# Output tiles of a second layer moved to other places in on-chip memory: four places for even chunks, four for odd ones, and a fifth store tile

## The chip, the core and the metric

The kernel runs on one core of a Trainium2 chip. A core has a matrix engine (PE), three elementwise engines (DVE, ACT, POOL) and a queue that only issues transfers (SP); each engine works through its own instructions strictly in order and waits on semaphores. SBUF is the on-chip memory of 128 partitions, and a tile takes the same range of bytes in each of them. The metric is device time in microseconds (us), the median of several runs; lower is better.

## The reference, cut to what matters

The input is one sequence of 4096 rows of 640 numbers. A modulation vector is made from `c`; then come a spectral block and a gated feed-forward block, each added to the residual:

```python
sa, ca, ga, sb, cb, gb = (silu(c) @ w_mod) cut in six
h = layernorm(x) * (1 + ca) + sa
x = x + ga * A(h)
h = layernorm(x) * (1 + cb) + sb
x = x + gb * ((silu(h @ w_gate) * (h @ w_up)) @ w_down)

def A(x):                              # along the 4096 rows
    z = rfft(x), its 640 channels cut in 4 blocks of 160
    h = relu(z @ w1 + b1)              # complex, per block
    o = h @ w2 + b2                    # complex, per block: the "second layer"
    o = sign(o) * max(|o| - 0.01, 0)   # real and imaginary part apart: "shrink"
    return irfft(o)
```

## The kernel before

**The spectral block, first part.** The transform of 4096 is split in 128 x 32. The input lies in eight tiles `xa0` to `xa7` (pool `xp`), each 10240 bytes of a partition, one after the other. Each is normalized, multiplied on PE by the constant `fa`, copied back over itself, and stored to memory by `write_s1(t, f)` in three shares f = 0, 1, 2 of its rows; I call such a store (t, f). These stores stand in SP's queue among loads, in the order of the code: (5,1), (0,1), (6,1), (7,1), (5,2), load of `g2` and `tb2`, (6,2), (7,2), and last (0,2); then the small constants `idn`, `tx`, `bx`, and then the first rows of `w_mod` (`wm`, L543). A tile's place is free for others when its stores have landed.

**The chunks.** The frequencies are worked in eight chunks `ch`, each with four channel blocks `b`, all in an order written out by hand; a step `p` is 4·ch + b. `stage_b` (L631, tile `pb`) is the second half of the transform; `evac_b` and `evac_r` copy it out as `z` and `rz` (ACT L638 and L661, DVE L639 and L671); `stage_l1` (L727, `pl`) is the first layer, whose results ACT (L744, L745) and DVE (L746, L759) take to `h` and `u`; `stage_l2` (L795, `pc`; for the first block also L792 and L806) is the second layer. DVE adds its bias and writes the sum to the output tiles `tts[ch, q, b // 2]` (named tt or tu): L807 for the first block, L797 for all others. `shrink_parts` (ACT L815 into the scratch tile `cl`, L816 in place) and `shrink` (DVE L819) apply the threshold. `stage_i` (L837, `pi`) is the first half of the inverse transform with the constant `bx`; ACT copies it to the four store tiles `co` (L840), which go to memory (`s2`) by POOL's queue (L845, and L843 for the last chunk). `first_blocks` runs chunk 0 and starts chunk 1; the loop over p follows.

Tiles that `stage_l2`, `shrink` and `stage_i` use lie in pool `p2`, which is laid over the places of `xp`. Who uses a place first waits for whoever used it before; the framework derives these waits from addresses. In bytes of a partition:

| place of | bytes | pool `p2` before |
|---|---|---|
| xa0 | 116672–126912 | nothing |
| xa1 | 126912–137152 | acc, cl, wx, bx, start of w2a |
| xa2, xa3 | 137152–157632 | w2a, w2b, start of w2c |
| xa4 | 157632–167872 | end of w2c, first tt place (chunk 0: q 0, b 0 and 1) |
| xa5 | 167872–178112 | four tt places (two used in chunk 0) |
| xa6 | 178112–188352 | a tt place (chunk 0: q 1, b 0 and 1), wm, two co places |
| xa7 | 188352–198592 | two co places, xn0, xn1 |

**The feed-forward block.** Its pool `fp` is laid over the same bytes. Its first step, `first_g`, transposes four normalized rows (`pt`, L1875), and per k writes the high part `ht` (ACT L1877), a copy `hx` (ACT L1880 for k < 3, DVE L1882 for the others) and the low part (DVE L1883); PE multiplies in the order k by k (L1889, L1890 with the high part, L1891 with the low one, tile `pg`). `hx0_0` lies at 186368, where before the last chunk's store tiles `co7_2` and `co7_3` lie. After that PE runs almost without a pause to the end (row 350.00:1451.00 of the prediction).

Of the kernel before, what the change touches and what calls it, by code (L numbers as in the profile page):

```python
# [6 lines left out]
F32 = mybir.dt.float32  # L7
# [6 lines left out]
P = 128  # L14
D = 640
# [151 lines left out]
def body(tc, x, w1, b1, w2, b2, wg, wu, wd, c, wm, k_fa, k_tb, k_tx, k_bx, k_ga, k_ge, k_id, out, dbg=None):  # L167
# [29 lines left out]
    with ExitStack() as top:  # L197
# [34 lines left out]
        with ExitStack() as af:  # L232
# [288 lines left out]
            p2 = af.enter_context(tc.tile_pool(name="p2", bufs=1, side="right", reuse_waits="tile"))  # L521
# [96 lines left out]
            tts = {}  # L618
# [154 lines left out]
            def stage_l2(ch, b, then=()):  # L773
                h0, h1, r2, _ = hss[ch, b]
                late = []
                de = slice(160 * (b % 2), 160 * (b % 2) + 160)
                for q in range(3 if ch == CE else 2):
                    fs = slice(128 * q, 128 * q + 128) if q < 2 else slice(256, 258)
                    M = 128 if q < 2 else 2
                    W = 320 if q < 2 else 160  # L780
                    if b % 2 == 0 and q < 2:
                        tts[ch, q, b // 2] = p2.tile([P, 2, 320], F32, tag="tt", bufs=6, name=f"tt{ch}_{q}_{b // 2}")
                    pc = ps.tile([P, 512], F32, tag="p2" if q < 2 else "p1", name=f"pc{ch}_{b}_{q}")
                    seq = [(h0[:, 0, fs], w2a[:, b, 0:W]), (h0[:, 1, fs], w2a[:, b, 0:W]),
                           (h0[:, 0, fs], w2a[:, b, 320:320 + W]),
                           (h1[:, 0, fs], w2b[:, b, 0:W]), (h1[:, 1, fs], w2b[:, b, 0:W]),
                           (h1[:, 0, fs], w2b[:, b, 320:320 + W]),
                           (r2[:, fs], w2c[:, b, 0:W]), (r2[:, fs], w2c[:, b, 320:320 + W])]
                    if (ch, b) == (0, 0):
                        late.append((pc, [seq[k] for k in (2, 5, 7)]))  # L790
                        for i, k in enumerate((0, 1, 3, 4, 6)):
                            mm(pc[:M, :W], *seq[k], start=(i == 0), stop=False)  # L792
                        continue
                    for i, (l, m) in enumerate(seq):
                        mm(pc[:M, :W], l, m, start=(i == 0), stop=(i == len(seq) - 1))  # L795
                    if q < 2:
                        dve.tensor_tensor(tts[ch, q, b // 2][:, :, de], pc[:, :320].rearrange("p (r e) -> p r e", r=2),  # L797
                                          b2t[:, :, b, :], op=OP.add)
                        if then:
                            then[q]()  # L800
                    else:

                        dve.tensor_tensor(tts[ch, 0, b // 2][0:1, 1, de], pc[0:1, :160], b2t[0:1, 0, b, :], op=OP.add)
                for q, (pc, seq) in enumerate(late):
                    for i, (l, m) in enumerate(seq):
                        mm(pc[:, :320], l, m, start=False, stop=(i == 2))  # L806
                    dve.tensor_tensor(tts[ch, q, b // 2][:, :, de], pc[:, :320].rearrange("p (r e) -> p r e", r=2),  # L807
                                      b2t[:, :, b, :], op=OP.add)

            cos = {}  # L810
# [14 lines left out]
            def stage_i(ch, hf, tag=("p1", "p1", "p3", "p3")):  # L825
                e = slice(320 * hf, 320 * hf + 320)
                if hf == 0:
                    cos[ch] = [p2.tile([P, D], F32, tag="co", bufs=4, name=f"co{ch}_{j}") for j in range(4)]
                co = cos[ch]
                pi = [ps.tile([P, 512], F32, tag=tag[j], bufs=1 if tag[j][0] == "b" else 2, name=f"pi{ch}_{hf}_{j}")  # L830
                      for j in range(4)]
                for r in range(2):
                    for q in range(2):
                        for j in range(4):
                            k = slice(32 * j, 32 * j + 32)
                            kd = 0 if 4 * ORDER[ch] + j + q == 0 else 1
                            mm(pi[j][64 * q:64 * q + 64, :320], bx[k, kd, r, :], tts[ch, q, hf][k, r, :],  # L837
                               start=(r == 0), stop=(r == 1))
                for j in range(4):
                    act.activation(co[j][:, e], pi[j][:, :320], AF.Copy)  # L840
                    m = 4 * (4 * ORDER[ch] + j)
                    if ch == NCH - 1:
                        (pool if hf else nc.scalar).dma_start(s2[m:m + 4, :, e].rearrange("k n d -> (k n) d"), co[j][:, e])  # L843
                    elif hf:
                        pool.dma_start(s2[m:m + 4].rearrange("k n d -> (k n) d"), co[j])  # L845

            on = lambda f, p, *a: f(p // 4, p % 4, *a) if 0 <= p < NP else None
            inverse = lambda p: stage_i(p // 4, p % 4 // 2) if p >= 0 and p % 2 == 0 else None

            e32 = hp.tile([P, 5, 2], F32, name="e32")  # L850
# [29 lines left out]
            def first_blocks():  # L880
# [19 lines left out]
                stage_l1(0, 2, later)  # L900
                stage_b(0, 3)
                stage_l2(0, 0)
                evac_b(0, 3)
                evac_rh(0, 3)
                stage_l2(0, 1, (lambda: evac_rl(0, 3), lambda: None))
                for f in later:
                    f()
# [5 lines left out]
                tail_l1(0, 3)  # L913
                evac_r(1, 0)
                stage_l2(0, 2)
                stage_b(1, 1)
                evac_b(1, 1)
# [5 lines left out]
            for p in range(LAST + 1):  # L923
                ch, b = p // 4, p % 4
# [75 lines left out]
            for p in range(LAST + 1, NP):  # L1000
                if p == LAST + 1:
                    on(shrink, p - 4)
                elif p == LAST + 3:
                    on(shrink_v, p - 3)
                    on(shrink_v, p - 2)
                on(stage_l1, p)
                on(tail_l1, p)
                if p < LAST + 3:
                    on(shrink_v, p - 3)
                if p == LAST + 1:  # L1010
                    load_first_rows(rb - 16, rb, nc.sync)
                elif p == LAST + 2:
                    load_first()
                    first_gate()
                for f, *a in sums.get(p, ()):
                    f(*a)
                if p == LAST + 1:
                    stage_i(NCH - 2, 0)
                on(stage_l2, p - 1)
                if p == LAST + 2:  # L1020
                    stage_i(NCH - 2, 1)
                    load_first_rows(rb, rb + 16, nc.sync)
# [74 lines left out]
        with ExitStack() as ff:  # L1097
# [15 lines left out]
            for n, (k, p) in enumerate(WG):  # L1113
                STG.append(("w", n))
                if k == "g" and p:
# [26 lines left out]
            bufs = {"R": 2, "h1": 1, "wb": 2, "wt": 3, "wd": 1, "wdh": 2, "wdl": 2, "pc": 4, "px": 2, "gt": 2, "ho": 2,  # L1142
                    "h32": 1, "sg": 4, "s": 5, "gx": 2, "rb0": 1, "rb1": 1, "ra0": 1, "ra1": 1, "m": 4, "e": 2}
# [1266 lines left out]
            mv, rs, _ = fst[3]  # L2410
# [22 lines left out]
            for t in range(NS):  # L2433
                for n in range(NW):
                    if sum_at(n) == t:
                        a, b = sum_w(n)
# [77 lines left out]
```

## Time and profile before

| | us |
|---|---|
| median of 3 runs (1451.87 to 1454.89) | 1454.39 |
| the profiled execution's time | 1453.16 |
| its span, first to last instruction | 1451.0 |
| PE busy | 1403.8 |
| DVE, ACT, POOL busy | 1080.9, 772.5, 536.9 |
| mean granted PE clock, share of full speed | 0.993 |

The rows of the timelines read: start in us, length, engine, line, operation, output tile, inputs, count, and in brackets the idle time ahead of it with what ended that. Rows of waits read: who waited for whom, the sum in us, how often, the longest. A table of windows gives busy time and count for PE, PEld (weight loads), DVE, ACT and POOL, then the granted PE clock and the share of the DMA engines.

### The profile page before, as it was taken

How to read it: one execution, taken by the hardware profiler on the slowest of the kernel's cores; microseconds unless marked ns; L12 is line 12 of the kernel's file. 1: busy time of each engine (PE TensorE's matmuls, PEld its weight loads, DVE VectorE, ACT ScalarE, POOL GpSimd, SP SyncE). 2: the span in 40 equal slices, each digit the busy share in tenths (PEclk: the TensorE clock that was granted, in tenths of full speed). 3: DMA queues.
4: the chain of work that ended last, by engine and by line, in shares of the span. 5: the costliest groups of instructions: out<-in, count | busy, mean ns of one | idle time of the engine just before them, and what ended most of it. 6: DMA issues, size and time to landing. Idle time of an engine off the chain costs nothing.

```text
span 1451.0 us, 24366 instructions
## 1 busy us (share of the span) xinstructions
PE 1403.8 (97%) x8828; PEld 1316.1 (91%) x8828; DVE 1080.9 (74%) x1947; ACT 772.5 (53%) x1538; POOL 536.9 (37%) x640
## 2 busy tenths in 40 slices
PE   7869999998999999999999999999999999999999
PEld 2668989967898888899999999999999999999999
DVE  8847777767888687857887868888747767567775
ACT  7837777736555455545465555555534444245432
POOL 5300122034354353423344434344324545146543
PEclk9979999999999999999999999999999999999999
DMA  9944677736766989898787997788796666966652
GB/s 376 321 175 163 211 223 262 225 129 207 277 242 222 360 294 301 284 373 273 261 280 241 318 397 235 261 289 271 280 343 218 228 205 236 368 212 238 205 180 94
DMA packets 182793, 372.88 MB, mean 257 GB/s; under 512 B 21360, under 2 KB 103856, under 8 KB 180880
## 3 DMA queue, kind: packets, MB, share of 16 engines
q1 hardware_dynamic: 174624, 355.19, 70.7%
q0 software_dynamic: 6464, 13.50, 2.8%
q10 hardware_dynamic: 1584, 2.62, 0.5%
q8 instruction: 70, 1.15, 0.3%
q14 instruction: 51, 0.42, 0.1%
HBM read 266.40 MB, written 104.86 MB: 256 GB/s over the span
## 4 chain that ended last, share of the span: by engine, by line
PE 83%; DVE 7%; DMA 5%; ACT 3%; issue 1%; POOL 1%; SPq 1%; ACTq 0%; DVEq 0%; POOLq 0%
PE pd L2384 15%; PE pw L2065 8%; PE pw L2067 8%; PE pw L2066 8%; PE pc L795 5%; PE pd_X L2246 5%; PE pl L727 4%; PE pg L1930 4%; PE pg L1929 4%; PE pg L1931 4%; PE pd_Y L2246 2%; PE pw L2076 2%; PE pw L2078 2%; PE pw L2077 2%; PE pb L631 2%; PE py L1651 2%
## 5 line engine op out<-in xcount | busy, mean ns | idle before, releaser
L2384 PE MATMUL pd<-wdh,a 128*128 128x320 f32 x1040 | 239.1, 310 | 0.6 <-DVE x L2356 0.6
L2384 PEld LDWEIGHTS pd<-wdh,a 128*128 128x128 f32 x1040 | 176.2, 188 | 1.2 <-DVE x L2356 0.9
L2384 PE MATMUL pd<-wdl,a 128*128 128x320 f32 x540 | 166.2, 309 | 0.0
L1406 DVE TENSOR_TENSOR wb<-r,wb 128x512 fp32r<-128x512 f32 (+3 forms) x154 | 152.6, 1001 | 12.2 <-ACT wb L1403 10.8
L2065 PE MATMUL pw<-h,wt 128*128 128x384 f32 x416 | 141.2, 339 | 2.2 <-ACT s_x L2084 2.2
L2067 PE MATMUL pw<-h,wt 128*128 128x384 f32 x416 | 140.2, 337 | 0.0
L2066 PE MATMUL pw<-h,wt 128*128 128x384 f32 x416 | 139.9, 336 | 0.0
L2356 DVE TENSOR_TENSOR x<-x,pd 128x320 f32<-128x320 f32 x240 | 109.5, 480 | 36.9 <-PE pd L2384 32.9
L1403 ACT ACTIVATE wb<-r 128x512 fp32r<-128x512 f32 (+3 forms) x170 | 117.4, 704 | 33.7 <-PE pw L2078 23.7
L2065 PE MATMUL pw<-h,wb 128*128 128x384 f32 x312 | 105.1, 337 | 0.9 <-DVE x L2356 0.9
L2066 PE MATMUL pw<-h,wb 128*128 128x384 f32 x312 | 104.6, 335 | 0.0
L2067 PE MATMUL pw<-h,wb 128*128 128x384 f32 x312 | 104.6, 335 | 0.0
L1929 PE MATMUL pg<-ht,wb 128*128 128x512 f32 x260 | 102.3, 393 | 0.0
L2384 PEld LDWEIGHTS pd<-wdl,a 128*128 128x128 f32 x540 | 101.4, 188 | 0.3
L1930 PE MATMUL pg<-ht,wb 128*128 128x512 f32 x260 | 101.4, 390 | 0.0
L1931 PE MATMUL pg<-ht,wb 128*128 128x512 f32 x260 | 101.4, 390 | 0.0
L2084 ACT ACTIVATE s_x<-pw 128x384 f32<-128x384 f32 x52 | 25.4, 489 | 120.3 <-PE pw L2067 119.2
L1634 POOL TENSOR_TENSOR cr<-cr,gab 128x640 f32<-128x640 f32 x28 | 46.6, 1667 | 98.3 <-DMA cr<-s 72.7
L2065 PEld LDWEIGHTS pw<-h,wt 128*128 128x128 f32 x416 | 78.1, 188 | 3.6 <-ACT s_x L2084 3.5
L2066 PEld LDWEIGHTS pw<-h,wt 128*128 128x128 f32 x416 | 78.2, 188 | 0.0
L2067 PEld LDWEIGHTS pw<-h,wt 128*128 128x128 f32 x416 | 78.1, 188 | 0.0
L845 POOL DMA_DIRECT2D s<-co x28 | 15.5, 555 | 161.4 <-ACT co L840 160.6
(348 smaller groups left out, 3976.4 us busy)
## 6 DMA issues: line engine op xcount, KB each, us to landing
wt<-td SPq DMA_DIRECT2D x104, 512.0 KB, 5.2
hs<-ho SPq DMA_DIRECT2D x52, 512.0 KB, 5.5
h<-hs SPq DMA_DIRECT2D x32, 768.0 KB, 9.3
r<-in_B_w_up_dram SPq DMA_DIRECT2D x36, 640.0 KB, 5.0
r<-in_B_w_gate_dram SPq DMA_DIRECT2D x36, 640.0 KB, 5.1
wdr<-wdd SPq DMA_DIRECT2D x25, 640.0 KB, 5.3
td<-wt SPq DMA_DIRECT2D x25, 512.0 KB, 5.4
g<-s SPq DMA_DIRECT2D x7, 1280.0 KB, 6.9
```

What stands on the lines that cost most here:

```text
L795: mm(pc[:M, :W], l, m, start=(i == 0), stop=(i == len(seq) - 1))
L1403: act.activation(wbs[t, n][:, 0, ks, e], raw[t, n][:, ks, e], AF.Copy)
L1406: (pool if onp else dve).tensor_tensor(wbs[t, n][:, 1, ks, e], raw[t, n][:, ks, e], f32(wbs[t, n][:, 0, ks, e]), op=OP.subtract)
L1929: mm(b, wh, hh, start=(kk == 0), stop=False)
L1930: mm(b, wh, hl, start=False, stop=False)
L1931: mm(b, wl, hh, start=False, stop=(kk == 4))
L2065: mm(b, w(0, kp), a[:, kp, 0], start=start and kp == 0, stop=False, skip_group_check=not start)
L2066: mm(b, w(0, kp), a[:, kp, 1], start=False, stop=False, skip_group_check=not start)
L2067: mm(b, w(1, kp), a[:, kp, 0], start=False, stop=kp == 1, skip_group_check=not start)
L2246: mm(bk[b, i][:, :320], x, y, start=new and j == 0, stop=j == len(seq) - 1, skip_group_check=not new)
L2356: dve.tensor_tensor(x2[:, e], x2[:, e], x[0][:, :320], op=OP.add)
L2384: mm(pd[g, hf][0][:, :320], l, m, start=i == 0, stop=i == len(s) - 1 and not (last and len(gs) > 1))
```

## The change

Two lines of the pool's tags change. The output tiles had one tag with six places, taken in turn; now even chunks take turns in four places `tt` and odd chunks in four places `tu`. The store tiles `co` have five places in place of four.

```diff
@@ stage_l2
                     if b % 2 == 0 and q < 2:
-                        tts[ch, q, b // 2] = p2.tile([P, 2, 320], F32, tag="tt", bufs=6, name=f"tt{ch}_{q}_{b // 2}")
+                        tts[ch, q, b // 2] = p2.tile([P, 2, 320], F32, tag=("tt", "tu")[ch % 2], bufs=4, name=f"tt{ch}_{q}_{b // 2}")
@@ stage_i
                 if hf == 0:
-                    cos[ch] = [p2.tile([P, D], F32, tag="co", bufs=4, name=f"co{ch}_{j}") for j in range(4)]
+                    cos[ch] = [p2.tile([P, D], F32, tag="co", bufs=5, name=f"co{ch}_{j}") for j in range(4)]
```

The pool grows by 7680 bytes, downwards, and so everything in it shifts:

| place of | pool `p2` now |
|---|---|
| xa0 | acc, cl, wx, bx |
| xa1, xa2, xa3 | w2a, w2b, w2c, one on each |
| xa4 | the four tt places (all of chunk 0) |
| xa5 | wm, three co places |
| xa6 | two co places, two tu places (chunk 1: q 0 and 1) |
| xa7 | two tu places, xn0, xn1 |

`hx0_0` now lies on places of tu tiles of chunk 7, and `hx0_2` to `hx0_4` on no store tile.

No engine's instructions change or move; what changes is what some of them wait for. In the rows below a wait is named by its semaphore: PE, DVE, Activation and Pool are the engines' own, DMAHW0 to DMAHW7 are eight counters that the transfers of SP and ACT take in turn, DMASW0 to 7 those of POOL's transfers. At DVE, where chunk 0's first block gets its output tiles (tt_0_0 and tt_1_0 are q 0 and q 1; `pc` the second layer's products):

```order
-L807 TENSOR_TENSOR tt_0_0_809<-pc_0_0_810,b2t 128x2x160 [waits DMAHW3_49,PE_49]
-L807 TENSOR_TENSOR tt_1_0_816<-pc_0_1_817,b2t 128x2x160 [waits DMAHW7_49,DMAHW0_49,PE_49]
+L807 TENSOR_TENSOR tt_0_0_809<-pc_0_0_810,b2t 128x2x160 [waits DMAHW2_49,DMAHW3_49,DMAHW1_49,PE_49]
+L807 TENSOR_TENSOR tt_1_0_816<-pc_0_1_817,b2t 128x2x160 [waits PE_49]
 L639 SCALAR_TENSOR_TENSOR z_3_831<-pb_3_804,ca_71,z_3_831 128x2x256 [waits Activation_49]
```

The second write waited for the stores (6,1) and (6,2) of xa6; now the first one waits for the stores (4,1) and (4,2) of xa4, and the second for nothing but PE. At ACT, the first shrink of the loop, with the copy of `z` ahead and chunk 1's first layer behind:

```order
 L638 ACTIVATE z_2_961<-pb_2_956,ca_71 128x2x256 [waits PE_49]
-L815 ACTIVATE cl<-tt_0_0_809,nlam 128x640 [waits DMAHW7_49]
-L816 ACTIVATE tt_0_0_809<-tt_0_0_809,nlam 128x640 [waits Activation_49]
+L815 ACTIVATE cl<-tt_0_0_809,nlam 128x640 [waits DMAHW7_49,DMAHW3_49]
+L816 ACTIVATE tt_0_0_809<-tt_0_0_809,nlam 128x640 [waits DMAHW2_49,DMAHW5_49,DMAHW1_49,Activation_49]
 L744 ACTIVATE h_1_0_0_981<-pl_0_0_971,b1m 128x256 [waits PE_49]
```

`cl` waited for the store (1,2); on xa0's place it waits for (0,1) and, by DMAHW3, for (0,2), the last of all those stores. On SP the load of `bx` (L536) gains the same wait for (0,2), with the first two loads of `wm` queued behind it. At ACT, the head of the feed-forward block:

```order
 L1877 ACTIVATE ht_3_3904<-pt_0_3930,sb_74,cb_73 128x512 [waits PE_49]
-L1880 ACTIVATE hx_0_3920<-pt_0_3930,sb_74,cb_73 128x512 [waits DMAHW6_49,DMASW7_49,DMAHW7_49,DMASW6_49,Activation_49]
+L1880 ACTIVATE hx_0_3920<-pt_0_3930,sb_74,cb_73 128x512
 L1877 ACTIVATE ht_5_3905<-pt_1_3931,sb_74,cb_73 128x512 [waits PE_49]
-L1880 ACTIVATE hx_1_3959<-pt_1_3931,sb_74,cb_73 128x512
+L1880 ACTIVATE hx_1_3959<-pt_1_3931,sb_74,cb_73 128x512 [waits Activation_49]
```

`hx0_0` waited for the last chunk's stores `co7_2` and `co7_3` on POOL's and ACT's queues; now it waits for none. Those waits stand later now: on ACT at the first `wdh` (L1577, for co7_1 and co7_2), at the second `wdh` (for co7_0) and at `sgr` (L1897, for co7_3).

## Prediction

> **What bounds the kernel now.** I read the table of windows first, since the share of busy time is a mean over stages with different limits.
>
> ```profile
> 114.00:300.00 186.00, 183.79 (x1687) 169.85 (x1683) 136.92 (x249) 137.79 (x289) 31.91 (x53) 1.00 0.65 212
> 350.00:1451.00 1101.00, 1090.53 (x6485) 1055.50 (x6483) 826.07 (x1429) 538.24 (x1069) 454.20 (x492) 1.00 0.77 266
> ```
>
> The second column is the length, the third PE's busy time. PE works for 99% of both stretches, at full clock: there the kernel is as long as its matmuls, and the change leaves these alone. What can move are the two stretches in between, 0 to 114 and 300 to 350 us; whatever time is taken off there, PE's next long run starts that much sooner. The waits of 60 to 112 us come next (who waited for whom: sum, times, longest):
>
> ```profile
> DVE tt L807 <- DMA s<-rst: 11.5, 1, 11.5
> ...
> PE pc L795 <- DVE tt L807: 10.5, 1, 10.5
> ...
> PE pc L792 <- POOL w2b L275: 3.0, 1, 3.0
> ```
>
> One wait of DVE for a store stopped PE. The timelines of DVE and PE put it in place:
>
> ```profile
> 75.02 0.49 DVE L807 TENSOR_TENSOR tt<-pc,b2t 128x320 f32<-128x320 f32 x1 [0.79 <-PE pc L806]
> 87.00 0.49 DVE L807 TENSOR_TENSOR tt<-pc,b2t 128x320 f32<-128x320 f32 x1 [11.48 <-DMA s<-rst]
> ...
> 87.55 1.17 PE L795 MATMUL pc<-w2a,h 128*128 128x320 f32 x3 [10.54 <-DVE tt L807]
> ```
>
> The second L807 is the write of tt_1_0 on xa6's place. It waited for that tile's stores, not for work: its matmuls stand ahead of PE's pause, which began at 87.55 − 10.54 = 77.0. In that pause stood PE, whose next product needed the bank that this write empties. The second stretch shows the same pattern:
>
> ```profile
> 325.90 0.78 ACT L1877 ACTIVATE ht<-pt,sb,cb 128x512 fp32r<-128x512 f32 x1 [1.27 <-PE pt L1875]
> 329.17 0.78 ACT L1880 ACTIVATE hx<-pt,sb,cb 128x512 f32<-128x512 f32 x1 [2.49 <-DMA s<-co]
> ...
> 329.98 2.03 DVE L1883 TENSOR_TENSOR ht<-hx,ht 128x512 fp32r<-128x512 f32 x2 [4.50 <-ACT hx L1880]
> ...
> 331.31 0.79 PE L1891 MATMUL pg<-ht,wh 128*128 128x512 f32 x1 [3.85 <-DVE ht L1883]
> ```
>
> ACT waits 2.49 us for the last chunk's stores, DVE for ACT, and PE 3.85 us for DVE.
>
> **The first term: chunk 0's output tiles.** The new places take the 11.48 us wait away: the stores of xa4, which the first tt write waits for now, are the last of the four in the first row below, issued by 57.9. So I look for what is late next, and find it on ACT: `cl` now lies on xa0's place, whose last store (0,2) is the last of them all. Rows of SP, with the times from issue to landing that the DMA view gives for (0,2) and `bx` alone and for `wm`:
>
> ```profile
> 55.47 2.43 SPq L345 DMA_DIRECT2D s<-xa  x4
> ...
> 82.15 0.99 SPq L345 DMA_DIRECT2D s<-xa  x1
> ...
> 85.53 0.38 SPq L536 DMA_DIRECT2D bx<-in_k_bx_dram  x1
> 86.89 0.84 SPq L543 DMA_DIRECT2D wm<-in_w_mod_dram  x2
> ...
> s<-xa SPq DMA_DIRECT2D x1, 640.0 KB, 8.3
> ...
> bx<-in_k_bx_dram SPq DMA_DIRECT2D x1, 128.0 KB, 5.5
> ...
> wm<-in_w_mod_dram SPq DMA_DIRECT2D x6, 320.0 KB, 4.8
> ```
>
> (0,2) lands at 82.15 + 8.3 = 90.45. It depends only on SP's queue, which is the same up to it, so I leave it there. ACT's row for the first use of `cl`, and what follows in its queue:
>
> ```profile
> 100.37 0.69 ACT L638 ACTIVATE z<-pb,ca 128x512 fp32r<-128x512 f32 x1
> 100.95 0.82 ACT L815 ACTIVATE cl<-tt,nlam 128x640 f32<-128x640 f32 x1
> 101.81 0.83 ACT L816 ACTIVATE tt<-tt,nlam 128x640 f32<-128x640 f32 x1
> ...
> 107.23 0.95 ACT L661 ACTIVATE rz<-pb,ca 32x256 fp32r<-32x256 f32 x2 [1.05 <-DVE rz L671]
> ```
>
> When would ACT come to L815 without the stall? It comes there after PE's first layer of the fourth block, which follows the stalled product; so at 100.95 − 10.54 = 90.41 at the latest. It is sooner if the 3.0 us wait for `w2b` goes too: POOL's second-layer weights waited for stores of xa2 and xa3 and now wait for those of xa1 and xa2, issued earlier; then 87.4. The slow clock after the stall (below) goes as well. All of that is worth nothing beyond 90.45: ACT stands at L815 until (0,2) has landed, with all its later work behind it, and DVE and PE behind that. From L815 on ACT is busy without a break but for 1.05 us, in which it waits for DVE, which had waited for ACT. So the whole chain to
>
> ```profile
> 108.22 1.00 DVE L671 SCALAR_TENSOR_TENSOR rz<-pb,ca,rz 32x256 fp32r<-32x256 f32 x2 [1.02 <-ACT rz L661]
> ...
> 105.53 0.52 PE L727 MATMUL pl<-z,w1a 128*128 128x256 f32 x3
> ...
> 109.27 2.05 PE L631 MATMUL pb<-tb,g 128*128 128x128 f32 x16 [1.06 <-DVE rz L671]
> ...
> 112.90 1.32 PE L837 MATMUL pi<-tt,bx 32*64 32x320 f32 x26 [0.29 <-DVE u L759]
> ```
>
> moves by 100.95 − 90.55 = 10.4 us (0.1 for the start after the landing, as at 87.00), and PE's full stretch begins at 112.90 − 10.4 = 102.5. Ends for this term: 7.5 if the store lands 3 us later (an estimate, a third of its 8.3), 16 if the wait on `cl` did not count (10.54 + 3.0 + 2.4 for the slow clock).
>
> **The clock.** Windows of 3.41 us, as long as the clock's own steps, show when PE is slowed (the third column from the end is the granted clock):
>
> ```profile
> 68.44:71.85 3.41, 0.57 (x4) 0.57 (x5) 2.11 (x3) 3.33 (x7) 3.41 (x3) 1.00 0.98 331
> 71.85:75.26 3.41, 3.16 (x11) 2.54 (x11) 2.62 (x3) 0.94 (x2) 1.59 (x3) 0.50 1.04 410
> 75.26:78.68 3.42, 1.75 (x10) 1.27 (x9) 0.25 (x1) 0.00 (x0) 0.00 (x0) 1.00 0.61 243
> 78.68:82.09 3.41, 0.00 (x0) 0.00 (x0) 0.00 (x0) 0.00 (x0) 0.00 (x0) 0.50 0.87 288
> ...
> 105.98:109.40 3.42, 2.36 (x20) 2.15 (x19) 2.11 (x6) 2.30 (x6) 0.00 (x0) 1.00 0.00 0
> 109.40:112.81 3.41, 3.21 (x22) 2.11 (x22) 3.38 (x8) 3.33 (x7) 0.00 (x0) 1.00 0.18 34
> ```
>
> A window with PE busy 1.75 of 3.42 us is followed by half clock, one with 2.36 is not. The change makes such a window: PE's first layer of chunk 1's second block (row 105.53, ended 108.2) needs only banks that ACT empties early, so it starts before −10.4 would put it, ends about 95.7, and PE then pauses 3.2 us up to `pb` at 98.9. Half clock from there for 3.4 us would make PE lose 1.7, of which about 1.2 lie beside DVE's work ahead of row 112.90 (2 us of `pb` and 6 of the `pi`, 0.3, in 3.6). I take −0.4 as what is left, with ends 0 and −1.7. The Trainium skill, page "TensorE: Matmul & The Clock Gate", Part 1, has another rule: half clock comes after an idle window of about 3.4 us, full clock after a busy one. By that rule the 3.2 us pause costs nothing; but the row 75.26:78.68 above is half busy and was followed by half clock, so the trace disagrees.
>
> **The second term: the head of the feed-forward block.** `hx0_0` loses its wait for the stores, so ACT goes on at 326.7 and DVE's low parts, which follow ACT one by one, start 2.49 us sooner. PE needs the first of them at 327.5, so it still waits, some 1.4 us. What is late next is DVE beside POOL:
>
> ```profile
> 332.65 1.99 DVE L1883 TENSOR_TENSOR ht<-hx,ht 128x512 fp32r<-128x512 f32 x1 [0.65 <-ACT hx L1880]
> ...
> 335.40 0.69 DVE L1883 TENSOR_TENSOR ht<-hx,ht 128x512 fp32r<-128x512 f32 x1
> ...
> 332.54 1.55 POOL L1634 TENSOR_TENSOR cr<-cr,gab 128x640 f32<-128x640 f32 x1 [1.84 <-DMA cr<-s]
> ...
> 331.26:334.67 3.41, 3.37 (x8) 2.69 (x9) 2.71 (x3) 3.41 (x7) 2.07 (x2) 0.50 0.93 314
> ```
>
> The same subtraction takes 1.99 us beside POOL's product and 0.69 alone. That product waits for a load behind the same stores, so it stays; it will meet a later low part and cost DVE the same 1.3. Half clock here (last row) cost PE 1.7 of matmuls, which may go with the shorter pause, but PE then waits for DVE's later low parts. So 2.5 us; ends 0 (POOL's product holds the last low part back by as much as was won) and 4.2 (2.5 + 1.7). The stores' waits now stand at the first `wdh`, more than 10 us after the landing that released ACT at 329.17.
>
> **Edits at nothing.** The fifth `co` place and the tu places only make waits older: the copies to `co` already waited for PE alone,
>
> ```profile
> 127.58 1.43 ACT L840 ACTIVATE co<-pi 128x320 f32<-128x320 f32 x4 [0.67 <-PE pi L837]
> ```
>
> and chunk 1's tu tiles wait for stores ahead of (0,2), some 10 us before their use. If a store took that much longer they would stall DVE by the rest. On SP, `bx` now waits for (0,2): it is issued 4.9 us later and lands at 90.5 + 5.5 = 96.0 at the worst, before its first use at 111.26 − 10.4 = 100.9 (the first `pi` follows `pb`: 109.27 + 1.99). The two `wm` loads behind it are issued by 91.8 and land by 96.6; DVE uses the first at
>
> ```profile
> 110.51 0.55 DVE L548 TENSOR_SCALAR acc<-wm,sc 128x640 f32<-128x640 f32 x1
> ```
>
> that is, at 100.1.
>
> **The sum.** 10.4 − 0.4 + 2.5 = 12.5 us. On the profiled execution's own time, 1453.16 − 12.5 = 1440.7. That execution lies 1.2 under the median of 1454.39 and inside the runs' spread, so on the median: 1441.9. Fewer than 3 us (0.2%) would not be told from no change.
>
> **Rivals.**
> - No half clock at `pb`: 10.4 + 2.5 = 12.9, so 1441.5. For it: the pause is not surely inside one window. Against it: the row 75.26:78.68. The skill's rule named above would give this time.
> - The second term is covered by DVE beside POOL: 10.0, so 1444.4. For it: the 1.99 us row; against it: the product cost DVE its 1.3 before as well.
> - `cl`'s wait does not count: 16 + 2.5, so 1436. It needs (0,2) to land by about 85, 3 us after its issue, while the DMA engines were busy 0.87 and more; the rows speak against it.
> - Nothing gained, 1454: the time won is given back where PE waits later. The two PE rows of 99% leave no wait large enough.
> - Slower: the same wait of ACT, with a late store. Before, nothing waited for (0,2) until long after; now L815 does, and everything with it. From 100.95 on, a landing 10.5 us later than the row's, the first term turns into a loss, and past 103.5 the second no longer pays for it. With a landing at 106.5 the kernel would be at 1454.4 + 5.5 − 2.5 = 1457.4. Speaking for it: the DMA engines are busy 0.87 and more while (0,2) waits. Against it: it took 8.3 with the same transfers ahead, and nothing is put ahead of it.
>
> **How the numbers follow.** My forecast 0.52, no half clock 0.25, second term covered 0.13, `cl` not counting 0.04, nothing gained 0.03, slower 0.03. So faster 0.94, same 0.03, slower 0.03. The first three lie between 1441.5 and 1444.4; the ends of the first term (a store 3 us later: +2.9) and of the second (4.2: −1.7), and the spread of 1.5 us either way of the runs, widen that to 1438 to 1447.
>
> **What the profile after would show.** L807 twice without a pause near 72 us; ACT idle some 3 to 5 us ahead of the first L815, ended by a store, with L815 near 90.6; PE's `pb` near 98.9 and perhaps one window at 0.50 after it; L1880 straight after L1877, PE's pause ahead of L1891 down from 3.85 to about 1.4; PE's busy time as before. The forecast is wrong if (0,2) lands at another time, if something else than `cl` holds ACT there, or if PE pauses anew after 350 us.

## The result and the profile after

The changed kernel takes 1442.18 us (median of 4 runs, 1439.0 to 1443.11) beside 1454.16 for the kernel before: ratio 0.9916, 95% interval 0.9897 to 0.9935. Run again beside the experiments it took 1442.01 against 1453.78, ratio 0.9916 (0.9902 to 0.9929). The forecast was 1441.9. The profiled execution took 1442.69, with a span of 1440.6.

The two long stretches of PE, the counterpart of the first table of the prediction: the first is laid 12 us earlier, the second runs again from 350 us to the end of the span, which comes some 10 us sooner:

```profile
102.00:288.00 186.00, 184.04 (x1699) 169.06 (x1698) 137.21 (x250) 137.24 (x287) 30.03 (x49) 1.00 0.65 211
350.00:1440.00 1090.00, 1080.23 (x6424) 1046.89 (x6422) 812.47 (x1415) 530.99 (x1056) 448.06 (x484) 1.00 0.77 266
```

PE is as full in them as before (99%), so the gain came from the gaps. The waits of 60 to 112 us in the profile after:

```profile
DVE tt L819 <- ACT tt L816: 4.9, 1, 4.9
ACT cl L815 <- DMA s<-xa: 4.2, 1, 4.2
...
PE pb L631 <- DVE rz L671: 3.1, 1, 3.1
```

The wait of DVE L807 (11.5) and that of PE L795 for it (10.5) are gone; ACT's wait at `cl` stands in their place. The timelines of after, engine by engine (DVE, SP, ACT, PE):

```profile
72.81 0.49 DVE L807 TENSOR_TENSOR tt<-pc,b2t 128x320 f32<-128x320 f32 x1 [0.79 <-PE pc L806]
73.61 0.49 DVE L807 TENSOR_TENSOR tt<-pc,b2t 128x320 f32<-128x320 f32 x1 [0.31 <-PE pc L806]
...
82.50 0.99 SPq L345 DMA_DIRECT2D s<-xa  x1
...
91.13 0.33 SPq L536 DMA_DIRECT2D bx<-in_k_bx_dram  x1
...
86.21 0.69 ACT L638 ACTIVATE z<-pb,ca 128x512 fp32r<-128x512 f32 x1
91.14 0.83 ACT L815 ACTIVATE cl<-tt,nlam 128x640 f32<-128x640 f32 x1 [4.24 <-DMA s<-xa]
...
99.46 3.64 PE L631 MATMUL pb<-tb,g 128*128 128x128 f32 x16 [3.08 <-DVE rz L671]
103.03 1.37 PE L837 MATMUL pi<-tt,bx 32*64 32x320 f32 x32
104.33 0.71 PE L795 MATMUL pc<-w2a,h 128*128 128x320 f32 x3
```

Read it downwards. DVE writes both tiles without waiting for a store. SP issues the store (0,2) at 82.50; at 91.13, 8.6 us later, `bx` is issued, which waited for the landing, and at 91.14 ACT starts L815, having stood idle since 86.90. Everything behind it keeps its distance: `pb` at 99.46 was at 109.27 before, 9.81 earlier, as L815 is (100.95 to 91.14).

The windows around `pb`:

```profile
92.58:96.00 3.42, 2.39 (x20) 2.40 (x21) 2.61 (x5) 3.33 (x9) 0.00 (x0) 1.00 0.61 201
96.00:99.41 3.41, 0.38 (x4) 0.17 (x2) 2.14 (x5) 2.33 (x5) 0.00 (x0) 1.00 0.00 0
99.41:102.82 3.41, 3.36 (x16) 3.37 (x16) 3.36 (x8) 2.89 (x7) 0.00 (x0) 0.50 0.13 20
```

The half clock came, in the third row, and DVE worked 3.36 us of it.

The head of the feed-forward block:

```profile
316.68 0.78 ACT L1877 ACTIVATE ht<-pt,sb,cb 128x512 fp32r<-128x512 f32 x1 [1.28 <-PE pt L1875]
317.36 0.77 ACT L1880 ACTIVATE hx<-pt,sb,cb 128x512 f32<-128x512 f32 x1
...
323.17 2.03 DVE L1883 TENSOR_TENSOR ht<-hx,ht 128x512 fp32r<-128x512 f32 x1
...
323.10 1.56 POOL L1634 TENSOR_TENSOR cr<-cr,gab 128x640 f32<-128x640 f32 x1 [1.24 <-DMA cr<-s]
...
317.51 0.50 PE L1889 MATMUL pg<-ht,wh 128*128 128x512 f32 x1 [0.43 <-ACT ht L1877]
...
319.35 0.50 PE L1891 MATMUL pg<-ht,wh 128*128 128x512 f32 x1 [1.10 <-DVE ht L1883]
...
325.26 0.50 PE L1891 MATMUL pg<-ht,wf 128*128 128x512 f32 x1 [1.15 <-DVE ht L1883]
...
327.74 0.39 PE L1929 MATMUL pg<-ht,wb 128*128 128x512 f32 x1
```

L1880 follows L1877 at once; PE's first pause is down from 3.85 to 1.10 us, and a second of 1.15 stands where POOL's product meets DVE's low part, which then takes 2.03 us. From the first L1889 to the first L1929 PE needs 10.23 us; before it was 12.73, between these two rows of the kernel before:

```profile
326.73 0.50 PE L1889 MATMUL pg<-ht,wh 128*128 128x512 f32 x1 [0.43 <-ACT ht L1877]
...
339.46 0.40 PE L1929 MATMUL pg<-ht,wb 128*128 128x512 f32 x1
```

### The profile page after: what moved, and what is told of

Same layout as the page of the kernel before. It is cut to its first block, busy times and chain, and to the rows that moved or that the text cites. A ratio compares the mean times of both kernels' runs of the same rounds, so it can differ in the third digit from the quotient of the medians.

```text
span 1440.6 us, 24366 instructions
## 1 busy us (share of the span) xinstructions
PE 1402.9 (97%) x8828; PEld 1316.0 (91%) x8828; DVE 1078.9 (75%) x1947; ACT 772.5 (54%) x1538; POOL 537.5 (37%) x640
## 3 DMA queue, kind: packets, MB, share of 16 engines
q10 hardware_dynamic: 1584, 2.62, 0.5%
q8 instruction: 70, 1.15, 0.3%
## 4 chain that ended last, share of the span: by engine, by line
PE 80%; DVE 9%; DMA 4%; ACT 3%; issue 2%; POOL 1%; SPq 1%; DVEq 0%; ACTq 0%; POOLq 0%
PE pd L2384 14%; PE pw L2065 8%; PE pw L2067 8%; PE pw L2066 8%; PE pd_X L2246 5%; PE pc L795 4%; PE pl L727 4%; PE pg L1930 3%; PE pg L1929 3%; PE pg L1931 3%; PE pd_Y L2246 3%; PE pw L2076 2%; PE pw L2078 2%; PE pw L2077 2%; PE pb L631 2%
## 5 line engine op out<-in xcount | busy, mean ns | idle before, releaser
L2384 PE MATMUL pd<-wdh,a 128*128 128x320 f32 x1040 | 240.4, 311 | 0.6 <-DVE x L2356 0.6
L2384 PEld LDWEIGHTS pd<-wdh,a 128*128 128x128 f32 x1040 | 177.3, 189 | 1.2 <-DVE x L2356 0.8
L2384 PE MATMUL pd<-wdl,a 128*128 128x320 f32 x540 | 166.8, 310 | 0.0
L2384 PEld LDWEIGHTS pd<-wdl,a 128*128 128x128 f32 x540 | 102.1, 189 | 0.3
L1929 PE MATMUL pg<-ht,wb 128*128 128x512 f32 x260 | 102.3, 393 | 0.0
L2220 DVE TENSOR_TENSOR x<-x,pd_X 128x320 f32<-128x320 f32 x144 | 64.4, 483 | 14.2 <-PE pd_X L2246 14.2
```

The lines of the kernel that those rows point to most:

```text
L1929: mm(b, wh, hh, start=(kk == 0), stop=False)
L2220: dve.tensor_tensor(x2, x2, q[:, :320], op=OP.add)
L2384: mm(pd[g, hf][0][:, :320], l, m, start=i == 0, stop=i == len(s) - 1 and not (last and len(gs) > 1))
```

## The experiments

Theory: two gates stand ahead of the long stretch, DVE's second L807 (until the stores of its tile's place have landed) and ACT's L815 (until (0,2) has landed); whichever ends last sets everything behind it, one for one. The feed-forward head is a second, separate term. Rival for each: the wait only coincides with another limit.

The table gathers the profiled execution of every kernel (us): the start of the second L807, the start of L815 and in brackets ACT's wait there for a store, PE's first L1889, the time from there to PE's first L1929, and from there to the end of the span. The last column is the median of 4 or 5 runs. Where DVE's rows stand together as x2, the second start is taken as the end of the pair less 0.49.

| kernel | 2nd L807 | L815 (wait) | L1889 | head | rest | median |
|---|---|---|---|---|---|---|
| before | 87.00 | 100.95 (0) | 326.73 | 12.73 | 1111.5 | 1454.16 |
| after | 73.61 | 91.14 (4.24) | 317.51 | 10.23 | 1112.9 | 1442.18 |
| after, again | 72.96 | 90.77 (5.11) | 316.98 | 9.43 | 1114.1 | 1442.01 |
| (0,2) ahead of (6,2) | 72.58 | 86.71 (1.44) | 312.45 | 9.43 | 1113.5 | 1437.67 |
| (7,2) stored twice | 72.58 | 94.13 (7.38) | 320.56 | 9.42 | 1112.4 | 1444.74 |
| tu below co | 72.77 | 91.07 (4.10) | 317.25 | 11.95 | 1112.1 | 1443.06 |
| fifth store tile alone | 78.69 | 90.78 (0) | 316.97 | 10.69 | 1112.7 | 1442.14 |
| tags alone | 78.56 | 90.61 (0) | 316.81 | 9.43 | 1112.7 | 1441.61 |
| (0,2) ahead of (6,2), again | 71.99 | 86.89 (0.82) | 313.23 | 10.22 | 1113.5 | 1437.25 |
| (0,2) ahead of g2 | 72.53 | 86.56 (0) | 312.95 | 9.99 | 1111.1 | 1437.16 |

The repeat of the changed kernel and the three rows below it were timed beside 1453.78 of the kernel before, the last four rows beside 1454.94.

**The changed kernel again.**

> The changed kernel once more, beside the others of this call: 1442.2 us within 1.5, L815 near 91.1 at the landing of (0,2). If the pause of 1.93 us at PE L2076 near 689 us belongs to the change it is there again; if it is chance of one execution it is not.

ACT and PE of this profile, with which the next runs are compared:

```profile
90.77 0.83 ACT L815 ACTIVATE cl<-tt,nlam 128x640 f32<-128x640 f32 x1 [5.11 <-DMA s<-xa]
...
99.10 3.50 PE L631 MATMUL pb<-tb,g 128*128 128x128 f32 x16 [3.09 <-DVE rz L671]
```

1442.01 us (1439.9 to 1442.93). The pause at L2076 is there again (1.95 us at 690.02), but it is in the kernel before as well (1.90 at 700.33): it belongs neither to the change nor to chance. What is chance is told below, in the part on the clock.

**The store (0,2) earlier.** The other two stores are issued behind it; nothing else changes.

```diff
-            for t in (6, 7, 0):
+            for t in (0, 6, 7):
                 write_s1(t, 2)
```

> The changed kernel with the store (0,2) issued ahead of (6,2) and (7,2), right after the loads g2 and tb2. Theory: the wait of cl for (0,2) is what sets the first term, one for one. Then (0,2) is issued near 79.6 in place of 82.5, lands near 88 (8.3 to 8.6 later), ACT, free at 86.9, runs L815 at 88, PE's pb starts near 96.4 in place of 99.5, and the kernel takes 1442.2 - 3.1 = 1439.1 us. With the pause ahead of pb gone the window at half clock goes too, at no gain if it was hidden. Rival: another wait holds the chain there and the store only coincides; then L815 moves to 88 but pb stays within 1 us of 99.5 and the time at 1442.2.

Timelines of that kernel, SP, ACT and PE:

```profile
78.59 0.48 SPq L345 DMA_DIRECT2D s<-xa  x1
...
84.58 0.69 ACT L638 ACTIVATE z<-pb,ca 128x512 fp32r<-128x512 f32 x1
86.71 0.83 ACT L815 ACTIVATE cl<-tt,nlam 128x640 f32<-128x640 f32 x1 [1.44 <-DMA s<-xa]
...
95.04 3.66 PE L631 MATMUL pb<-tb,g 128*128 128x128 f32 x16 [2.62 <-DVE rz L671]
...
99.91 0.71 PE L795 MATMUL pc<-w2a,h 128*128 128x320 f32 x3
```

1437.67 us (1437.2 to 1438.59), ratio to before 0.9889 (0.9875 to 0.9902); its slowest run is below the fastest of the changed kernel. L815 moved by 4.06 against the repeat of the changed kernel, `pb` by 4.06 (99.10 to 95.04), the median by 4.34. The store landed 1.3 us sooner than I had expected, 1.0 of it because it was issued sooner (78.59 for 79.6). The pause ahead of `pb`, which I had expected to go, stayed (2.62), because it lies behind L815 and moved with it. The rival, in which `pb` stays, is out.

**The store (0,2) later.**

```diff
-            for t in (6, 7, 0):
+            for t in (6, 7, 7, 0):
                 write_s1(t, 2)
```

> The changed kernel with the store (7,2) issued a second time ahead of (0,2), which delays (0,2). Theory: one for one. The second issue waits for the first to land, so (0,2) is issued near 90 and lands near 96 to 98; L815 stands at the landing, 5 to 7 us later than in the changed kernel, pb as much later, and the kernel takes 1447 to 1449.5 us. Rival: the chain has slack behind L815, so that a later landing costs clearly less than it moves L815; then 1442 to 1445.

```profile
90.59 0.63 SPq L345 DMA_DIRECT2D s<-xa  x1
...
86.06 0.69 ACT L638 ACTIVATE z<-pb,ca 128x512 fp32r<-128x512 f32 x1
94.13 0.83 ACT L815 ACTIVATE cl<-tt,nlam 128x640 f32<-128x640 f32 x1 [7.38 <-DMA s<-xa]
...
102.44 2.05 PE L631 MATMUL pb<-tb,g 128*128 128x128 f32 x16 [1.56 <-DVE rz L671]
...
107.31 0.71 PE L795 MATMUL pc<-w2a,h 128*128 128x320 f32 x3
```

The dose was smaller than expected: issued at 90.59, (0,2) landed in about 3.5 us in place of 8.6 (what the traces show of that is told at the end). So L815 is 3.36 later than in the repeat, PE's L795 3.34 later, and the median 2.73 higher: 1444.74 (1443.81 to 1446.86), where I had expected 1447 or more. One for one holds for the trace; in the median 0.6 is missing, less than the runs differ among themselves. From L815 to that L795 it is 13.20, 13.20 and 13.18 us in the repeat and these two, 13.19 in the first profile of after, and 100.95 to 114.14, 13.19, before; over all ten profiles it is 13.18 to 13.33. No run has slack there.

**Each edit alone.** First the fifth store tile without the new tags (the kernel before with `bufs=5` for `co`), then the tags without the fifth store tile (the changed kernel with `bufs=4`).

> The kernel before with the second edit alone, five co places; the output tiles keep one tag of six places. The pool grows downwards by 2560 bytes, so tt_1_0 comes to lie on xa5 and waits for the store (5,2), and cl does not lie on xa0. Theory: where the first tiles lie sets the early gain, whichever edit moves them. The store (5,2) lands near 79, so the second L807 runs at 79 in place of 87; L815 follows 13.3 to 14 us behind it, as it did before (87.00 to 100.95) and in the changed kernel, at 92.3 to 93, with no wait for a store; hx0_0 still waits for stores of the last chunk, but for ones issued sooner. In all 1443.5 to 1446 us. Rival: the tags alone make the early gain, and this edit only the one at the feed-forward block; then L815 stays near 101 and the time at 1450 to 1452.

> The changed kernel with the first edit alone, the tags; co has four places. The pool lies 2560 bytes higher, so tt_1_0 lies on xa5 and waits for (5,2), while cl still reaches into xa0 and waits for (0,2). Theory: DVE's wait for (5,2) ends near 79, which brings ACT to L815 at 92.3 to 93, later than the landing of (0,2) near 91; so the wait of cl is gone and L815 is 1.2 to 2 us later than in the changed kernel: 1443 to 1444 us. Rival: there is slack between L807 and L815, L815 stands at the landing and the time is that of the changed kernel, 1442; the fifth store tile would then be worth nothing.

DVE and ACT of the first:

```profile
78.69 0.49 DVE L807 TENSOR_TENSOR tt<-pc,b2t 128x320 f32<-128x320 f32 x1 [3.37 <-DMA s<-xa]
...
90.19 0.69 ACT L638 ACTIVATE z<-pb,ca 128x512 fp32r<-128x512 f32 x1
90.78 0.82 ACT L815 ACTIVATE cl<-tt,nlam 128x640 f32<-128x640 f32 x1
```

1442.14 us (1441.64 to 1443.9) and 1441.61 (1439.9 to 1442.72): each edit alone gives the whole gain, and both times the lower end of what I had expected was 1.4 us more. The wait of L807 ended where expected, near 78.6, and the wait of `cl` was gone as expected; but L815 followed at 90.78 and 90.61, 12.1 us behind L807, not 13.3 to 14. My distance came from profiles in which PE ran at half clock. From the second L807 to the point at which ACT is free for L815 it takes 13.3 to 14.2 us in the six profiles with a window at half clock at or just behind that L807, and 12.1 to 12.7 in the four without. So three arrangements meet at 91 by two different gates: the two edits together free L807 and then stand at the landing of (0,2), while either edit alone makes L807 stand at the landing of (5,2), and comes to L815 12.1 us behind that. That they meet is chance: with the tags alone, where `cl` still waits for (0,2), that store landed at 90.2 (issued at 82.03, 8.2 us), only 0.4 ahead of L815. The rival of the first, that the tags alone make the early gain, is out. In the second the time is the rival's, 1442, but not by its mechanism: L815 stood at no store. Once the tags are there, the fifth store tile adds nothing that the medians show.

**The store (0,2) ahead of g2**, beside the earlier version once more.

```diff
             write_s1(5, 2)
+            write_s1(0, 2)
             load_g(2)
             load_tb(2)
-            for t in (6, 7, 0):
+            for t in (6, 7):
                 write_s1(t, 2)
```

> The changed kernel with (0,2) ahead of (6,2) and (7,2) once more, beside the next one: 1437.7 us within 1.

> The changed kernel with (0,2) issued still earlier, ahead of the load g2, whose wait held SP's queue from 73.3 to 77.3 in the run with (0,2) after it. Theory: the store then lands near 81, ACT, free at 85.3, runs L815 without a wait for any store, and what is left of that wait, 1.4 us, is won: 1436.3 us. Rival: behind that wait the next limit stands already (DVE or PE, or g2 and the other two stores, which now come later), so that the time stays at 1437.7 or rises.

ACT of the second (its lines are numbered one higher):

```profile
85.97 0.69 ACT L639 ACTIVATE z<-pb,ca 128x512 fp32r<-128x512 f32 x1
86.56 0.82 ACT L816 ACTIVATE cl<-tt,nlam 128x640 f32<-128x640 f32 x1
```

1437.25 (1436.79 to 1438.98) and 1437.16 us (1436.13 to 1437.97). ACT waits for no store any more, but it comes to `cl` at 86.56, since the copy of `z` ahead of it ended only then. The 85.3 that I had expected came from the first run with (0,2) earlier. One difference stands in the windows behind the second L807, first of that run, then of this one:

```profile
71.32:74.73 3.41, 2.88 (x18) 2.65 (x19) 2.39 (x6) 0.11 (x1) 0.00 (x0) 1.00 1.03 400
```

```profile
72.54:75.95 3.41, 3.32 (x12) 3.32 (x13) 1.90 (x5) 0.00 (x0) 0.00 (x0) 0.50 1.05 406
```

In this run PE was at half clock there, in the other it was not. So the rival's time holds. That it was PE at half clock which kept ACT until 86.56 fits the two groups of distances above, but no run tests it, and whether the 1.4 us can be had in an execution without that window is not shown. The medians of the two versions lie 4.3 to 5 us below those of the changed kernel (the last four rows of the table were not timed beside it), and the kernel before is beaten by ratios of 0.988 (0.9866 to 0.9895) and 0.9879 (0.9863 to 0.9896).

**The second term undone.** Two tiles that are never used fix the order of the pool's places, so that the tu places come to lie below the co places:

```diff
+            p2.tile([P, 2, 320], F32, tag="tt", bufs=4, name="ttp")
+            p2.tile([P, 2, 320], F32, tag="tu", bufs=4, name="tup")
             acc = p2.tile([P, D], F32, name="acc")
```

> The changed kernel with the four tu places put below the five co places, so that chunk 0's tiles and cl stay where the change has them, but hx0_0, hx0_3 and hx0_4 lie on store tiles of the last chunk again. Theory: the second term is the wait of hx0_0 for those stores, and this takes it back; L815 stays near 91.1, PE's pauses ahead of L1891 grow again by 1 to 2.5 us, and the kernel takes 1443.2 to 1444.7 us. Rival: the second term was worth nothing, since DVE beside POOL or PE's clock set that stretch; then 1442.2.

ACT and PE of that kernel (its lines are numbered two higher), and its windows there:

```profile
317.82 0.78 ACT L1882 ACTIVATE hx<-pt,sb,cb 128x512 f32<-128x512 f32 x1 [0.63 <-DMA s<-co]
...
319.88 0.80 PE L1893 MATMUL pg<-ht,wh 128*128 128x512 f32 x1 [1.90 <-DVE ht L1885]
```

```profile
315.62:319.03 3.41, 1.84 (x11) 0.93 (x8) 0.77 (x2) 1.99 (x3) 3.31 (x6) 1.00 0.54 192
319.03:322.44 3.41, 2.56 (x6) 2.10 (x7) 3.26 (x4) 3.41 (x6) 2.17 (x4) 0.50 0.60 157
322.44:325.86 3.42, 3.42 (x9) 2.68 (x9) 3.35 (x5) 1.42 (x3) 2.03 (x2) 0.50 0.82 261
```

L815 stayed (91.07). The wait for the stores came back at 0.63 us, PE's pause grew by 0.8 (1.90 for 1.11), and two windows at half clock came with it: the head takes 11.95 us, 2.5 more than in the repeat. So in the trace the term is there, and the clock is the greater part of it. That part is in part chance of the execution: after a window with PE busy 1.84 us half clock followed here, and elsewhere did not (below), and with the fifth store tile alone the same pause of 1.90 us brought one window at half clock and a head of 10.69. In the median it shows as 1.05 us (1443.06, 1440.36 to 1444.85), and the two kernels' runs overlap: in the time alone the rival, no effect, is not excluded.

## Why the prediction was right, point by point

- **First term, 10.4.** Right in its mechanism: what is late next is ACT at `cl`, by the landing of (0,2). It measured 9.81 in the first profile and 10.18 in the repeat. The difference is the queue: I had taken SP's issue at 82.15 and 8.3 us to the landing as fixed; they were 82.50 and 8.6. ACT was free at 86.90 in the first profile and at 85.66 in the repeat, somewhat sooner than the 87.4 that I gave with the wait for `w2b` gone; that is 14.1 and 15.3 us ahead of 100.95, so the end of 16 us for a wait that does not count was a little too large. The experiments on the order of the stores show the term itself, in both directions.
- **The clock, −0.4.** The window at half clock came where it was foretold, and cost nothing: the stretch from L815 to L795 is 13.2 us with it (both profiles of after, and the first run with (0,2) earlier; 13.33 in the second) and 13.19 to 13.20 where the whole stretch is at full clock (the kernel before, each edit alone, (0,2) ahead of g2). With (7,2) stored twice and with tu below co the half clock came earlier in the stretch, and it took 13.18 and 13.19. The step that failed is the 0.4 taken as left over beside DVE: nothing of it reached L795. So the price was that of the first rival, though its condition, no half clock, did not hold. The Trainium skill, page "TensorE: Matmul & The Clock Gate", Part 1, has half clock after an idle window, and as the prediction read it this pause, of 3.08 us, would have brought none. The window it fell in, busy 0.38 us of 3.41, comes near to such an idle window; the window of 1.84 shown for the last experiment, also followed by half clock, does not fit that rule.
- **Second term, 2.5.** The head became shorter by 12.73 − 10.23 = 2.50 in the first profile and by 3.30 in the repeat. The pause ahead of L1891 gave 2.75 of it, and the rest of the head, without the window at half clock that stood there before, 0.9; the second pause took 1.15 back in the first profile and 0.33 in the repeat. The product of POOL met a later low part, as foretold: 2.03 us for 0.69 in the first profile. In the repeat it ran beside two, of which one kept its 0.69 and the last took 1.22, and the second pause of PE was 0.33 in place of 1.15. The rival that this cover takes the whole term is out by the table.
- **The sum, 12.5.** 9.81 + 0 + 2.50 = 12.3 by the terms; the spans differ by 10.4, the medians by 12.0. What lies between is in two places. From L815 to L1889 it takes 225.8 before and 226.4 after (225.7 to 226.4 over all runs). And the rest behind the head takes 1112.9 for 1111.5. I had held that no wait there was large enough to give anything back; 1.4 us did come back in this profile, and 2.6 in the repeat. It varies from 1111.1 to 1114.1 between the profiles and does not follow the edits, so part of it comes and goes with the execution; with one profile of the kernel before, how much of it is a price of the change is not shown. The clock makes some of it (below); short waits of PE for DVE and ACT are another part, in the repeat 1.14 us ahead of L2384, where the kernel before has 0.6. Why these come in one execution and not in another was not settled. So it is in part luck that the forecast lies 0.3 us from the median: the terms together were 12.3 and 13.5 us in the two profiles, and a loss that no term of the sum had took the surplus back.
- **Edits at nothing.** Right: `bx` was issued at 91.13, 5.6 us later, and PE's first `pi` came behind `pb` without a wait for it. No tu tile waited for a store.
- **Slower by a late store.** It did not happen, but the mechanism is real: with (7,2) stored twice the median is 2.7 us higher.

## What to carry to other kernels

When a wait at a reused place is removed, list the remaining waits by the time they end, not by their length: here the wait of 11.5 us hid one that ended 4 us later than the work needed, and the next 4.3 us were had by issuing one store ahead of two others in a queue. Since a free place comes with the last store that reads it, the order of the stores and the layout of the pool have to be chosen together. And a distance between two instructions is only carried over from a trace in which neither a wait nor a slow clock lies inside it.

## What the runs showed of the hardware

**A pause of PE costs by where it falls in the clock's windows.** The same pause of 1.9 us ahead of L2076 is in all ten profiles. The windows, laid on the edges at which the clock changed in the same execution, for before, after and the repeat of after:

```profile
696.49:699.90 3.41, 1.94 (x12) 1.62 (x10) 3.41 (x6) 0.53 (x2) 0.62 (x1) 1.00 0.40 154
699.90:703.31 3.41, 2.98 (x20) 2.98 (x21) 3.41 (x9) 2.51 (x7) 0.00 (x0) 1.00 0.93 280
```

```profile
686.49:689.90 3.41, 1.48 (x9) 1.16 (x8) 3.41 (x7) 0.90 (x2) 0.00 (x0) 1.00 0.60 184
689.90:693.31 3.41, 3.41 (x15) 3.40 (x14) 2.90 (x7) 3.16 (x7) 0.00 (x0) 0.50 1.05 375
```

```profile
685.84:689.26 3.42, 2.23 (x13) 1.91 (x11) 3.42 (x5) 0.20 (x1) 0.96 (x1) 1.00 0.38 147
689.26:692.67 3.41, 2.65 (x17) 2.65 (x18) 3.41 (x9) 2.51 (x7) 0.00 (x0) 1.00 0.88 257
```

A pause that lies whole in one window leaves 1.48 us busy there (1.46 to 1.53 over the five such profiles), and half clock follows; one that an edge cuts leaves 1.94 or more in each, and none follows. The edges lie elsewhere in each execution. Five of the ten profiles had the half clock there, and took 751.2 to 751.7 us from L2076 to the end of the span; the other five took 749.6 to 751.3, on average 0.8 less.

**Busy time in a window decides only outside a band.** Over the windows of all ten profiles from 62 to 700 us, taken at full clock: whenever PE was busy 1.53 us or less, half clock followed; whenever it was busy 1.94 or more, it did not. From 1.55 to 1.86 both were seen (half after 1.84 in the rows of the last experiment, none after 1.77 in the repeat of after), so something besides the busy time that these rows give counts there; what it is, no run tells. (In the first 7 us of the span the rows show full clock while PE is idle; they are left out.) At half clock more is asked: the window 319.03:322.44 above, busy 2.56 us, was followed by half clock again, and so was one of 2.53, while 3.36 (99.41:102.82 of after) was followed by full clock.

**The time to a landing goes by what else is moving.** The stretches from issue to landing of (0,2), first in the kernel with (7,2) stored twice, then in after:

```profile
90.60:94.10 3.50, 0.79 (x6) 0.52 (x4) 0.00 (x0) 0.00 (x0) 0.00 (x0) 1.00 0.93 324
```

```profile
82.50:91.10 8.60, 8.44 (x68) 8.23 (x67) 4.92 (x10) 2.90 (x6) 0.00 (x0) 1.00 0.95 326
```

The DMA engines were equally full and moved 324 and 326 GB/s (the last column), that is 1.1 MB in the one stretch and 2.8 MB in the other, for the same 640 KB. So a store issued 8.1 us later landed only 3.0 us later: what else the engines had to move, not its own size, set how long it took. That need not stand ahead of it in SP's queue: with (0,2) ahead of (6,2) and (7,2), and these two stores issued behind it, it still took 8.1 us, while 317 GB/s were moved.
